# Rows of h carried through the 2x2 scheme of o @ W': four blocks of the second pair

## The chip, the cores and the metric

The kernel runs on one core of one Trainium2 chip. The metric is the device time of one execution in microseconds, as the median over several runs. One core has five engines with instruction queues of their own: TensorE (PE in the profile, with its weight loads as PEld), VectorE (DVE), ScalarE (ACT), GpSimd (POOL) and SyncE (SP). Each works through its own list in the order in which the program wrote it and waits on semaphores for the others. In this kernel SP issues the plain transfers and POOL the accumulating ones, which add what they bring to what lies in the destination.

## The reference

One input x (2048 x 512) goes through two blocks, and a gate of one number per token mixes them:

```
g = sigmoid((x * gate_w).sum(-1))                     # one per token
A: q,k,v = x @ wqkv, 32 heads of 16; phi(t) = where(t>0, t+1, exp(t)) + 1e-6
   kv = sum_s phi(k) v ;  z = sum_s phi(k)
   o  = phi(q) kv / (phi(q) z + 1e-6) ;  a = o @ wo
B: h = (x @ w_gate) * (x @ w_up)                      # 2048 x 1792
   b = h @ w_down                                     # 1792 x 512
out = g * a + (1 - g) * b
```

All of it is in float32. The kernel folds kv into wo, so that `a = o @ W'` where o is phi(q) divided by its denominator (and, in this kernel, multiplied by the gate) and W' is a 512 x 512 matrix.

## The kernel before

**Exactness.** Every operand X of a large matrix product is split into a high part (rounded to the type float32r) and a low part (X minus the high part). A product is then three matmuls, high x high, high x low and low x high (`mm3`, line 60). A split is a ScalarE copy (`act`, L74) for the high part and a VectorE subtraction (`tt`, L77) for the low one. In the names of the profile the letter at the end tells which: `oh` and `ol` for o, `owh` and `owl` for W', `dh` and `dl` for w_down, `hh` and `hl` for h, `wch` and `wcl` for weight combinations.

**Phase 1** computes k, phi(k), the gate and the sum behind kv. It takes about 92 us and isn't touched, but for where the gate's numbers lie.

**Phase 2** goes over two pairs of 512-token chunks (1024 tokens, 8 tiles of 128 tokens, a pair). A pair has 16 units: 14 for the blocks of 128 columns of h (kind "f") and two for q (kind "q", each 256 columns). Units are counted here from 0 to 31 over both pairs. A unit computes two 128-column products for both chunks with seven products instead of eight (a Strassen scheme over a 2x2 split of x and of the weights). In a unit the products stand on TensorE in the order 2 (bank Y), 3 (X), 4 (Y), 1 (R), 5 (X), 6 (R), 7 (S); each is six matmuls 512 wide. Between them VectorE and ScalarE work: R = X - m2, t = R + cross, S = t - X, and at the end of an "f" unit h = R * cross and S * cross, split into hh and hl.

**Fillers.** Between those products stand other matmuls at four places of the unit: ahead of product 4, ahead of product 1, and twice ahead of product 6. `down(k)` puts k down jobs there, and behind them the o jobs that have become ready. `shares` says how many down jobs each place gets (one each where it says nothing).

- A *down job* multiplies one tile of 128 tokens of h, for a group of two neighbouring blocks of h, with w_down: 2 x 3 matmuls 512 wide (`pdn`). VectorE adds the result, times (1 - g), to `acc` (L80). There are 7 groups a pair, so 7 x 8 = 56 jobs.
- An *o job* is one row half of one of seven products of another 2x2 scheme (`OPROD`): o (1024 tokens x 512) and W' are cut into 2 x 2 blocks, and sums of blocks are multiplied. One job is twelve matmuls 256 wide (`po`). VectorE adds the results to the right quarters of `acc`.

**The order of the work around the o jobs** is written by hand in `o_products`. A step of it is one of the places "e" (behind product 3 of a unit), "c" (behind product 4), "t" (behind product 1) and "end" (behind product 7). Counted in steps of job k: the first block of o is loaded at k - 5 (SP), the further blocks are added by accumulating transfers at k - 3 (POOL), and at k the tile is split (`ready`) and the job queued for the next filler place that comes. For the weights of product p, with k = 2p: load at 2p - 5, add at 2p - 3, split at 2p - 1 (`w_split`).

Within a unit ScalarE's list is: m2, the high part of h of the unit before, the split of w_down, place "e", the copy of Y (`cross<-bY`), place "c", three pieces `wch<-wr` of the next unit's weights, two scalings `wr<-wr` of the weights after those (POOL's add `wr<-in_wgu_add` waits for them), place "t", the copy of X, place "s" (ahead of the last filler), the high part of h, place "end". VectorE has the matching list. Everything is pinned to program order.

**At the end** of the last unit stand the rest of the older down jobs, and then the eight jobs of the last group, the last of which closes each tile of the output.

Of the kernel before, what the change touches and what calls it, by code (L numbers as in the profile page):

```python
# [7 lines left out]
F32 = mybir.dt.float32  # L8
# [23 lines left out]
NH = 4  # L32
HALF = D // 2

# [21 lines left out]
STEPS = ("e", "c", "t", "end")  # L56
# [3 lines left out]
def gated_mix(ctx: ExitStack, tc, xt, xp, x, wqkv, wq, wq_add, wo, wgu, wgu_add, wdn, gate_w, out):  # L60
# [48 lines left out]
    ocol = const.tile([P, NT], F32, name="ocol")  # L109
# [16 lines left out]
    nc.vector.memset(gate[:, NT:2 * NT], 0.0)  # L126
# [14 lines left out]
    gpark = dram.tile([NT, P], F32, name="gpark")  # L141
# [248 lines left out]
    def down(k):  # L390
        for fn in jobs[:k]:
            fn()
        del jobs[:k]
        while ojobs and ojobs[0][0] < passed[0]:
            ojobs.pop(0)[1]()
        passed[0] += 1
# [4 lines left out]
    shares = {2: (0, 1, 1, 1), 3: (1, 0, 1, 0), 4: (1, 0, 1, 0), 7: (1, 1, 0, 1), 8: (1, 0, 1, 0), 9: (1, 1, 0, 1)}  # L401
    shares.update({units: (1, 2, 1, 2), units + 1: (1, 1, 1, 0)})
    shares.update({units + m: v for m, v in ((2, (0, 1, 1, 1)), (3, (1, 0, 1, 0)), (4, (1, 0, 1, 0)),
                                             (5, (1, 1, 0, 1)), (6, (1, 1, 0, 1)), (7, (1, 0, 1, 0)),
                                             (15, (1, 1, 0, 0)))})
# [4 lines left out]
    def unit(n, quad):  # L410
# [38 lines left out]
        do(n, "low")  # L449
        do(n, "e")  # L450
# [31 lines left out]
        if quad:  # L482
            quad(1, 1, bank["R"])
        else:
# [5 lines left out]
        if quad:  # L490
            quad(0, 0, bank["S"])
        else:
# [19 lines left out]

    def hidden():
        return [p2.tile([P, 2, CH], F32R, tag=f"h{v}", name=f"h{v}", bufs=NH) for v in "hl"]

    def down_tiles():
        return [p2.tile([P, D], F32R, tag=f"d{v}", name=f"d{v}", bufs=NH + 1) for v in "hl"]

# [52 lines left out]
    def gate_rows():  # L571
# [3 lines left out]
        for q in range(0, P, 2 * NT):  # L575
            dma(gpark[:, q:q + 2 * NT], some[q:q + NT, 0:2 * NT])
# [44 lines left out]
    left = {(p, i): NF // 2 for p in range(NPAIR) for i in range(TPP)}  # L621
    oleft = [2 * len(OPROD) for _ in range(NPAIR)]

    def down_jobs(pair, group):

        def job(i):
# [6 lines left out]
            first = left[pair, i] == NF // 2  # L633
# [5 lines left out]
            for o in range(0, D, step):  # L639
# [3 lines left out]
                for j, ((hh, hl), w2) in enumerate(group):  # L643
                    mm3(pd, (hh[:, c, sl], hl[:, c, sl]), [v[:, cols] for v in w2], j == 0, j == 1)
# [5 lines left out]
                if ends:  # L650
                    to = nc.gpsimd if pair == 0 else nc.sync
                    tc.keep_in_program_order(to.dma_start(out[t * P:(t + 1) * P, cols], a))

# [279 lines left out]
```

## Time and profile before

| | |
|---|---|
| Median of 3 runs | 601.88 us (601.63 to 601.91) |
| Profiled execution | 601.07 us, of it the span 599.3 us |
| TensorE busy | 594.4 us (99% of the span), 2826 matmuls |
| VectorE, ScalarE, GpSimd busy | 457.2, 326.6, 70.3 us |
| Weight loads (PEld) | 496.0 us, beside the matmuls |
| Transferred | 113.40 MB, mean 189 GB/s |

How to read it: a timeline row gives the start in the span, the duration, the engine, the line, the operation and the tiles, written `out<-in`; behind that, in brackets, how long the engine had been idle and what released it. Durations of matmuls (and of VectorE and ScalarE steps in a row) overlap with those of their neighbours, so the distance from start to start is what one of them costs. A grouped row gives the count, the busy time, the mean duration and the idle time of the engine just before. "DMA to landing" is the time from the issue of a transfer until all of it has arrived.

### The profile page before, as it was taken

To read this page: it belongs to the slowest core of one execution; us is meant where nothing else is said; L and a number is where in the kernel's file an instruction comes from. 1 tells how busy PE (TensorE), PEld (TensorE's weight loads), DVE (VectorE), ACT (ScalarE), POOL (GpSimd) and SP (SyncE) were. 2 spreads that over 40 slices of the span, in tenths; PEclk is the share of its full clock that TensorE was granted. 3 is DMA by queue.
4 is the path that set the end of the run, shared out by engine and by line. 5 is a ranking of instruction groups with operands and counts; after the bars stand their busy time and mean duration, and the time that the engine had idled before them with its cause. 6 is when DMAs were issued, how large, how long until landed. Compare 5 with 4: busy or idle time off the path is not lost.

```text
span 599.3 us, 8138 instructions
## 1 busy us (share of the span) xinstructions
PE 594.4 (99%) x2826; PEld 496.0 (83%) x2826; DVE 457.2 (76%) x726; ACT 326.6 (54%) x569; POOL 70.3 (12%) x90
## 2 busy tenths in 40 slices
PE   8999999999999999999999999999999999999997
PEld 6888888888888888888888888888888888888886
DVE  6977895756787779777789986578768778788955
ACT  3855765579655844546345545955754445353320
POOL 0011100000011110222021121000000022210000
PEclk9999999999999999999999999999999999999999
DMA  8567949656959887999887974677784899965003
GB/s 294 180 194 127 289 102 274 167 167 159 262 135 294 206 211 186 288 267 232 188 179 198 238 202 117 162 177 184 207 215 106 231 249 239 236 174 92 1 1 141
DMA packets 62697, 113.40 MB, mean 189 GB/s; under 512 B 7680, under 2 KB 26624, under 8 KB 62592
## 3 DMA queue, kind: packets, MB, share of 16 engines
q1 hardware_dynamic: 51072, 76.18, 37.9%
q0 software_dynamic: 11296, 36.18, 34.0%
q10 hardware_dynamic: 288, 0.52, 0.3%
q8 instruction: 22, 0.36, 0.2%
q14 instruction: 19, 0.16, 0.1%
HBM read 95.03 MB, written 19.93 MB: 192 GB/s over the span
## 4 chain that ended last, share of the span: by engine, by line
PE 99%; DMA 1%; ACT 0%; DVE 0%; issue 0%
PE pdn L68 25%; PE bR L68 15%; PE bY L68 15%; PE bX L68 15%; PE pk L68 7%; PE bS L68 7%; PE gt L68 7%; PE po L68 7%; DMA wraw<-in_wqkv 1%; PE pw L68 0%; PE pkv L68 0%; ACT wkh L74 0%; DVE acc L80 0%
## 5 line engine op out<-in xcount | busy, mean ns | idle before, releaser
L80 DVE SCALAR_TENSOR_TENSOR acc<-pdn,ocol,acc 128x512 f32<-128x512 f32 (+1 forms) x97 | 71.6, 741 | 27.7 <-PE pdn L68 27.2
L68 PE MATMUL pdn<-dl,hh 128*128 128x512 f32 (+1 forms) x226 | 87.6, 388 | 0.0
L68 PE MATMUL pdn<-dh,hh 128*128 128x512 f32 (+1 forms) x226 | 87.6, 388 | 0.0
L74 ACT ACTIVATE hh<-cross 128x512 fp32r<-128x512 f32 x56 | 35.2, 629 | 96.0 <-DVE cross L77 96.0
L68 PE MATMUL pdn<-dh,hl 128*128 128x512 f32 (+1 forms) x226 | 87.5, 387 | 0.0
L77 DVE TENSOR_TENSOR wcl<-wr,wch 128x512 fp32r<-128x512 f32 (+1 forms) x96 | 73.3, 771 | 1.4 <-ACT wch L74 1.2
L74 ACT ACTIVATE wch<-wr 128x512 fp32r<-128x512 f32 (+1 forms) x96 | 60.2, 695 | 0.5 <-DMA wr<-in_wgu_add 0.5
L101 POOL DMA_DIRECT2D wr<-in_wgu_add x28 | 24.0, 858 | 249.2 <-ACT wr L74 136.0
L68 PE MATMUL bX<-xbh,wcl 128*128 128x512 f32 x128 | 49.8, 389 | 0.0
L68 PE MATMUL bX<-xbl,wch 128*128 128x512 f32 x128 | 49.8, 389 | 0.0
L68 PE MATMUL bX<-xbh,wch 128*128 128x512 f32 x128 | 49.8, 389 | 0.0
L68 PEld LDWEIGHTS pdn<-dh,hl 128*128 128x128 f32 x226 | 42.4, 188 | 8.8
L68 PEld LDWEIGHTS pdn<-dl,hh 128*128 128x128 f32 x226 | 42.5, 188 | 8.5
L68 PEld LDWEIGHTS pdn<-dh,hh 128*128 128x128 f32 x226 | 42.5, 188 | 8.5
L74 ACT ACTIVATE cross<-bY 128x512 f32<-128x512 f32 x32 | 19.1, 597 | 47.9 <-PE bY L68 47.7
L77 DVE TENSOR_TENSOR bR<-bX,m 128x512 f32<-128x512 f32 x32 | 22.3, 698 | 24.0 <-PE bX L68 21.1
L77 DVE TENSOR_TENSOR t<-bR,cross 128x512 f32<-128x512 f32 x32 | 22.1, 690 | 23.8 <-PE bR L68 15.2
L74 ACT ACTIVATE cross<-bX 128x512 f32<-128x512 f32 x32 | 19.1, 597 | 38.2 <-DVE bS L77 38.1
L77 DVE TENSOR_TENSOR hl<-cross,hh 128x512 fp32r<-128x512 f32 x56 | 38.2, 683 | 0.6
L74 ACT ACTIVATE wr<-wr 128x512 f32<-128x512 f32 x64 | 36.6, 621 | 2.0 <-DMA wr<-in_wq 1.9
L77 DVE TENSOR_TENSOR acc<-acc,po 128x512 f32<-128x512 f32 x40 | 26.3, 682 | 7.7 <-PE po L68 7.1
L68 PE MATMUL po<-owh,ol 128*128 128x256 f32 x112 | 31.7, 283 | 0.0
(175 smaller groups left out, 1470.5 us busy)
## 6 DMA issues: line engine op xcount, KB each, us to landing
wr<-in_wgu_add POOLq DMA_DIRECT2D x28, 640.0 KB, 7.6
wr<-in_wgu SPq DMA_DIRECT2D x28, 384.0 KB
wdr<-in_wdn SPq DMA_DIRECT2D x28, 256.0 KB
oraw<-opark POOLq DMA_DIRECT2D x20, 256.0 KB, 7.5
xraw<-in_x SPq DMA_DIRECT2D x16, 256.0 KB
terms<-zq SPq DMA_DIRECT2D x16, 256.0 KB
zt<-terms SPq DMA_DIRECT2D x16, 256.0 KB
rb<-den SPq DMA_DIRECT2D x16, 256.0 KB
```

What stands on the lines that cost most here:

```text
L68: tc.keep_in_program_order(nc.tensor.matmul(*args, **kw))
L74: pin(nc.scalar.activation(dst, src, func, **kw))
L77: pin(nc.vector.tensor_tensor(dst, a, b, op=op))
L80: pin(nc.vector.scalar_tensor_tensor(dst, a, scalar, b, op0=op0, op1=op1))
L101: tc.keep_in_program_order(nc.gpsimd.dma_start(dst, src, accum_op=ALU.add))
```

## The change

Four of the second pair's blocks of h (f = 4 to 7, `MIXED`) no longer go through down jobs. Their 512 columns are a second "o" of the same shape, and their rows of w_down a second "W'"; both go through the same seven products, which accumulate in the same banks. So each of the seven products of the second pair has two h jobs and then two o jobs, 28 instead of 14, and the second pair has 5 groups of down jobs instead of 7 (40 jobs).

- **Units of the mixed blocks** (22 to 25): h is written unsplit to `hraw`, and at place "low" of the next unit VectorE multiplies it with `keep`, (1 - g) broadcast over the partitions (two loads by SP). Its sums of blocks (`h_sum`) and its splits happen at the steps of the jobs.
- **Weights of an h job** are loaded from w_down itself, scaled by -1 on ScalarE where the scheme has a minus sign, and the second block is added by a POOL transfer. There are now 14 weight tiles instead of 7 in the second pair, at the same three steps 2j - 5, 2j - 3 and 2j - 1.
- **Steps**: the second pair has five a unit ("e", "c", "t", "s", "end") instead of four. Its second q unit is unit 21 instead of 22, its first unit 17 instead of 18 ("one place sooner"), and so step 0 lies at place "t" of unit 26 instead of unit 27. The 28 jobs end behind unit 31's "end".
- **Fillers**: `shares` is changed; units 18 and 26 of the second pair have no down job, units 22 and 25 one. The o jobs that are ready are now also put behind R = X - m2 (`o_down`), ahead of the place "e".
- **The end**: the two down jobs behind the last unit's product 7, `down(2)`, are gone, and the o/h jobs of steps 26 and 27 stand there.
- **Places**: h (hh, hl) and w_down (dh, dl in one tile) share nine tiles (`SLOTS`), each taken for the next free use once a group's last job is written, instead of 4 + 4 and 5 + 5 of their own. The split of w_down for the second block of a group moves from place "e" to behind the product of R ("r").
- **Gate**: (1 - g) lies in `gate` beside g, is transposed with it and stored too (8 small transfers instead of 4).

```diff
-NH = 4
+SLOTS = 9
+MIXED = ((), (4, 5, 6, 7))
-STEPS = ("e", "c", "t", "end")
+STEPS = (("e", "c", "t", "end"), ("e", "c", "t", "s", "end"))
...
-    for pair, after in enumerate(((2, 5), (1, 4))):
+    for pair, after in enumerate(((2, 5), (0, 3))):
...
-    shares = {2: (0, 1, 1, 1), 3: (1, 0, 1, 0), 4: (1, 0, 1, 0), 7: (1, 1, 0, 1), 8: (1, 0, 1, 0), 9: (1, 1, 0, 1)}
-    shares.update({units: (1, 2, 1, 2), units + 1: (1, 1, 1, 0)})
...
+    shares = {2: (0, 1, 1, 1), 3: (1, 0, 1, 0), 4: (1, 1, 0, 1), 7: (1, 1, 0, 1), 8: (0, 1, 0, 1), 9: (1, 1, 0, 1)}
+    shares.update({units: (1, 2, 1, 2), units + 1: (0, 1, 0, 1)})
+    shares.update({units + m: (0, 1, 0, int(m not in (6, 9))) for m in range(5, 10)})
...
         tt(bank["R"], bank["X"], m2, ALU.subtract)
         do(n, "low")
+        o_down()
         do(n, "e")
...
+        elif mixed:
+            tt(mixed[:, 1], bank["R"], cross[:, 1], ALU.mult)
...
+        def h_sum(k):
+            p, kind, r = line[k]
+            if kind == "h" and len(OPROD[p][2]) == 2:
+                one, other = OPROD[p][2]
+                tt(raw_tile(k), row(other, r), row(one, r), ALU.subtract if one[0] == "-" else ALU.add)
...
+        def w_sum(j):
+            p, kind, _ = line[2 * j]
+            if kind == "h" and OPROD[p][1][0][0] == "-":
+                act(wt[j], wt[j], scale=-1.0)
             for block in OPROD[p][1][1:]:
-                dma_add(wt[p], wraw[block])
+                dma_add(wt[j], w_block(p, kind, block))
...
+    def keep_scale(pair, m):
+        for c in range(2):
+            h = rows_of_h[pair, m][:, c]
+            tt(h, h, keep[c], ALU.mult)
...
+            mixed = rows_of_h[pair, m] = p2.tile([P, 2, CH], F32, tag="hraw", name="hraw", bufs=4)
+            later(n + 1, "low", lambda pair=pair, m=m: keep_scale(pair, m))
+        elif kind == "f" and half:
+            later(n, "r", down_weights)
...
-    down(2)
     do(n, "low1")
+    down(0)
     down(1)
     do(n, "low0")
     down(len(jobs))
```

More of the change, by code (lines that the diff above doesn't have):

```diff
@@ L741, in load @@
         def load(k):
[L742 to L743 removed]
+            p, kind, i = line[k]
+            if kind == "o":
+                dma(raw_tile(k).rearrange("p (r t) -> p r t", r=2), opark[pair, OPROD[p][2][0]][i])
         def add(k):
[L746 to L751 removed]
@@ L790, in o_products @@
+        last = len(line)
         for k in range(-5, last):
-            if k % 2 and (k + 1) // 2 in range(len(OPROD)):
+            if k % 2 and (k + 1) // 2 in range(last // 2):
                 at_step(k, lambda place, p=(k + 1) // 2: w_split(p))
```

158 lines of the change are left out of this document (106 added, 52 removed).

## The prediction

> **What bounds the kernel now.** I read the page's busy line and slices first, then its chain, then the matmul groups by shape.
>
> ```profile
> span 599.3 us, 8138 instructions
> PE 594.4 (99%) x2826; PEld 496.0 (83%) x2826; DVE 457.2 (76%) x726; ACT 326.6 (54%) x569; POOL 70.3 (12%) x90
> PE   8999999999999999999999999999999999999997
> PE 99%; DMA 1%; ACT 0%; DVE 0%; issue 0%
> L68 PE MATMUL pdn<-dh,hh 128*128 128x512 f32 x222 | 86.5, 389 | 0.0
> L68 PE MATMUL po<-owh,oh 128*128 128x256 f32 x112 | 31.6, 282 | 0.0
> ```
>
> TensorE is never idle between head and tail, and 99% of the chain is TensorE. So matmuls that go away are a gain in full, and any moment in which TensorE waits is a loss in full. The means of 389 and 282 ns are latencies that overlap; the cost of one is its distance to the next start:
>
> ```profile
> 560.05 0.28 PE L68 MATMUL po<-owh,oh 128*128 128x256 f32 x1
> 561.48 0.40 PE L68 MATMUL pdn<-dh,hh 128*128 128x512 f32 x1
> 565.69 0.39 PE L68 MATMUL bS<-xah,wch 128*128 128x512 f32 x1
> 569.77 0.39 PE L68 MATMUL pdn<-dh,hh 128*128 128x512 f32 x1
> ```
>
> Twelve 256-wide matmuls lie between the first two rows: 1.43/12 = 0.119 us each. Eighteen 512-wide ones lie between the last two: 4.08/18 = 0.227 us. So a product of a unit (six) and a down job (six) take 1.36 us each, an o job (twelve narrow ones) 1.43.
>
> **The change, part by part.**
>
> *Matmuls.* Four blocks leave the down jobs: 2 groups x 8 jobs x 6 = 96 wide matmuls, 96 x 0.227 = 21.8 us. Fourteen h jobs of twelve come in: 168 x 0.119 = 20.0 to 20.1 us. Net -1.7 us, all on the path. [...]
>
> *Units without filler.* Units 18, 21, 22 and 24 to 26 lose down jobs, so the next engine has less cover. I cost this at nothing where only the unit's own chain is concerned, because unit 0 of before has no filler either:
>
> ```profile
> 92.36 0.39 PE L68 MATMUL bY<-xah,wch 128*128 128x512 f32 x1
> 101.88 0.39 PE L68 MATMUL bY<-xah,wch 128*128 128x512 f32 x1
> ```
>
> It took 9.52 us = 42 x 0.227: no wait. The shared slots go at nothing with it: a group's last down job stands ahead of R6 on TensorE, and the new h is written behind R6. So do the keep loads. The q units' loads and stores move with them, and the units behind are up to 2.7 us shorter:
>
> ```profile
> L77 DVE TENSOR_TENSOR zt<-zt 128x512 f32<-128x512 f32 x12 | 8.2, 684 | 0.8 <-DMA zt<-terms 0.8
> 497.15 0.68 DVE L77 TENSOR_TENSOR t<-bR,cross 128x512 f32<-128x512 f32 x1
> 497.74 0.68 DVE L77 TENSOR_TENSOR wcl<-wr,wch 128x512 fp32r<-128x512 f32 x1
> ```
>
> VectorE's 0.8 us wait for zt may become 0.8 + 2.7; behind it stands t, which R6 of unit 19 needs 2.7 us (two down jobs) later than the bare chain has it, so 0. VectorE's load: its steps start 0.6 us apart (497.15, 497.74). Keep adds 8, the sums of h 10, the splits of o and W' 14 and 7; 16 sums into acc, 8 h splits and 4 w_down splits go. Units 26 and 27 together get 42 steps, 25 to 26 us, against 27.7 us of TensorE: not the bound, but without slack at job 0.
>
> *The first o/h product of the second pair: the first loss.* In unit 26 the order of the changed program is Y X Y R X, job 0, R, S, with nothing before job 0, where before had two down jobs. The same spot of before is unit 27, ScalarE, VectorE and TensorE:
>
> ```profile
> 493.67 0.39 PE L68 MATMUL pdn<-dh,hh 128*128 128x512 f32 x1
> 493.93 0.60 ACT L74 ACTIVATE cross<-bY 128x512 f32<-128x512 f32 x1 [2.44 <-PE bY L68]
> 495.21 0.63 ACT L74 ACTIVATE owh<-wraw 128x512 fp32r<-128x512 f32 x1 [0.69 <-DMA wraw<-wraw]
> 495.75 1.87 ACT L74 ACTIVATE wch<-wr 128x512 fp32r<-128x512 f32 x3
> 497.53 1.14 ACT L74 ACTIVATE wr<-wr 128x512 f32<-128x512 f32 x2
> 498.57 0.62 ACT L74 ACTIVATE oh<-oraw 128x512 fp32r<-128x512 f32 x1
> 499.22 0.69 DVE L77 TENSOR_TENSOR ol<-oraw,oh 128x512 fp32r<-128x512 f32 x1 [0.79 <-ACT oh L74]
> 500.47 0.28 PE L68 MATMUL po<-owh,oh 128*128 128x256 f32 x1
> ```
>
> The second Y ended at 493.67, ol at 499.91: 6.24 us, of which 0.69 was a DMA wait, so 5.55. ScalarE's order in unit 26 is the same row of seven: cross, owh, three wch, two wr, oh. Between the end of Y and the third matmul of job 0 (the first that reads ol) TensorE has only R, X and two narrow ones: 2.72 + 0.24 = 2.96 us. So it waits at least 5.55 - 2.96 = 2.6 us.
>
> On top comes owh's own wait for the weights, which the shorter units make longer:
>
> ```profile
> 478.97 0.60 ACT L74 ACTIVATE cross<-bY 128x512 f32<-128x512 f32 x1 [0.91 <-PE bY L68]
> 480.50 0.48 SPq L98 DMA_DIRECT2D wraw<-wraw x1
> 482.67 0.86 POOL L101 DMA_DIRECT2D wr<-in_wgu_add  x1 [14.10 <-DVE t L77]
> 484.84 0.86 POOL L101 DMA_DIRECT2D oraw<-opark  x1 [1.31 <-DMA wraw<-wraw]
> 485.48 1.10 POOL L101 DMA_DIRECT2D wraw<-wraw  x1
> DMA to landing us min/median/max: 8.7/8.7/8.7
> DMA to landing us min/median/max: 9.7/9.7/9.7
> DMA to landing us min/median/max: 5.8/5.8/5.8
> ```
>
> The landings are those of the wr add at 482.67, of the wraw add at 485.48 (behind it in POOL's queue: 491.4, then 495.2) and of a wraw add at 497.88 with less ahead. The wr add goes out 3.7 us after the cross copy. Unit 25 of the changed kernel is 8 x 1.36 = 10.9 us long; its cross copy comes at 4.3, the wr add at 8.0. The w load (SP, held behind the last store of o, about 6.2; 484.84 - 480.50 = 4.3 us to arrive) lets the w add go at 10.5. It lands between 10.5 + 5.8 = 16.3 and 8.0 + 8.7 + 1.9 = 18.6 (1.9: half of the 3.8 us between the two landings, as one o add lay between), 5.4 to 7.7 us into unit 26. ScalarE is ready for owh at 4.9. The wait is 0.5 to 2.8 us, and wch, wr and oh, then POOL's next wr add, queue behind it. First stall: 2.6 without it, up to 5.4; I take 4.2.
>
> *The next ones.* Jobs 1 and 2 stand together after X of unit 27. The second weight load takes keep's buffer, so SP holds it (and the loads behind it) till unit 26's keep products are done, 4.2 us in; 4.3 to load and 5.8 to add gives 14.4, and ScalarE's owh, oh and the sign change of the third weight block follow till 16.1. Only then goes that block's add: 5.8 more, 21.9 at best. Its owh, oh and ol (0.5 + 0.6 + 0.7 by the rows above) stand in order ahead of job 3's ol, ready at 23.7 or later; unhindered TensorE would be at job 3's third matmul at 18.1. So the lateness grows to 5.6, up to 7.5 if the wr add is ahead in POOL's queue. With no DMA late the sign change would end at 13.2, and 5.8 + 1.8 more is 20.8: 2.7. Sum of both stalls: 2.7 to 7.5, I take 6.2. From unit 28 on down jobs are back between the products; a step there has 22.2/5 = 4.4 us against 20.8/4 = 5.2 before, so I cost it at 0, at most 2.
>
> *The tail: the second loss.* Before covers the last h with three down jobs (the first at 580.75); the change has jobs 26 and 27 there, and job 27's o is split last:
>
> ```profile
> 579.66 0.69 DVE L77 TENSOR_TENSOR cross<-bR,cross 128x512 f32<-128x512 f32 x1 [0.73 <-ACT cross L74]
> 580.38 0.63 ACT L74 ACTIVATE hh<-cross 128x512 fp32r<-128x512 f32 x1 [0.82 <-DVE cross L77]
> 580.75 0.39 PE L68 MATMUL pdn<-dh,hh 128*128 128x512 f32 x1
> 580.95 0.69 DVE L77 TENSOR_TENSOR cross<-bS,cross 128x512 f32<-128x512 f32 x1 [0.60 <-PE bS L68]
> 581.67 0.63 ACT L74 ACTIVATE hh<-cross 128x512 fp32r<-128x512 f32 x1 [0.66 <-DVE cross L77]
> ```
>
> S ended at 580.75. In the changed order the split of w_down now lies between the two cross products: its copy on ScalarE ends at 581.5, its rest on VectorE at 582.2, cross at 582.8, hh at 583.5, oh at 584.0, ol at 584.7, 4.0 us after S. TensorE has job 26 (1.43) and two matmuls (0.24): it waits 2.3 us. Bounds: 1.2 without the w_down split in between (two steps, 1.1 us), 3 if VectorE is one step behind.
>
> *Sum.* -1.7 + 6.2 + 2.3 = +6.8 us. The profiled execution took 601.07 (span 599.3 and 1.77 around it), 0.81 under the median of 601.88. On the median: 608.7, said as 608.5. Ends: -1.7 + 2.7 + 1.2 = +2.2 (604.0) and -1.7 + 7.5 + 3 + 2 = +10.8 (612.7), with a margin 613.5.
>
> **The rivals.**
>
> *Everything stays covered: faster.* Then only the matmuls count: 601.88 - 1.7 = 600.2. For it: no row of before shows TensorE waiting for o. It decides at job 0 of unit 26: ol must be there 2.96 us after Y's end. The rows give 5.55 with no DMA late, so this needs ScalarE in another order than the program has. 0.09.
>
> *Only one of the two losses shows.* The tail alone: 601.88 - 1.7 + 2.3 = 602.5; the start alone at its low end 603 to 604. For it: VectorE has gaps at the tail (0.60 to 0.73 us in the rows). Against: both are in-order chains of single durations. 0.09, of which 0.05 ends within 0.2%.
>
> *The clock drops after the first stall.* The granted clock in the last moments, 3.1 us after the last matmul, and the first matmuls of the kernel:
>
> ```profile
> 595.90:599.00 3.10, 0.04 (x1) 0.00 (x0) 0.48 (x1) 0.00 (x0) 0.00 (x0) 1.00 0.46 169
> 599.00:599.30 0.30, 0.00 (x0) 0.00 (x0) 0.00 (x0) 0.00 (x0) 0.00 (x0) 0.56 0.00 0
> 1.26 3.59 PE L68 MATMUL warm<-xc1h 128*128 128x512 bf16 x8 [1.26 <-DVE xc1h L124]
> ```
>
> The first eight took 3.59/8 = 0.45 us each against 0.227. If TensorE sits idle for 3.9 us ahead of job 0 in one piece and then runs at that pace for as long, some 9 wide matmuls cost 0.2 more each: 1.8 us, and 610 to 612 if job 3 repeats it. [...] Against: two matmuls of job 0 split the gap, and the idle piece may be 2.6. 0.07, at 611.
>
> *The weight adds are late all through units 28 to 31.* Eight or more of fourteen by 1 us: 617. Against: the spacing is only 15% tighter than in before, which has no wait there. 0.05.
>
> **How the numbers follow.** Forecast 0.70 at 608.5, its own range 604 to 613.5. With the clock case that is 0.77 to 0.81 inside, the rest outside, so the range stays. 0.2% (1.2 us) is about what can be told from no change. Faster 0.09; same 0.05; slower 0.70 + 0.04 + 0.07 + 0.05 = 0.86.
>
> **What would show it.** PE matmuls: 96 wide fewer, 168 narrow more, at the same pitches. In the chain ScalarE and VectorE appear by 1% or more. TensorE's idle rows for po name VectorE's ol or ScalarE's oh: some 4 us at unit 26's job 0, about 2 in unit 27, 2.3 behind the last S. ScalarE's owh waits for wraw. [...]

## The result and the profile after

The changed kernel takes 619.43 us (median of four runs, 617.47 to 621.61) against 601.89 us before: 1.029 times as long, 95% interval 1.0255 to 1.0326. The direction was forecast, the size was not: 608.5 was said, and 619.4 lies outside 604 to 613.5.

The profiled execution is the slowest of the four, 621.61 us. From its page: the span, the busy line, two rows of the slices, the start of the chain, and the groups of matmuls for which TensorE waited.

```profile
span 619.6 us, 8338 instructions
PE 599.4 (97%) x2898; PEld 500.1 (81%) x2898; DVE 461.7 (75%) x736; ACT 332.9 (54%) x580; POOL 76.8 (12%) x95
PE   8999999999999989999999899999998789999987
PEclk9999999999999999999999999999999799999999
PE 86%; DVE 5%; DMA 5%; issue 2%; ACT 2%; ACTq 0%; DVEq 0%; POOLq 0%
L71 PE MATMUL pdn<-slot,slot 128*128 128x512 f32 (+1 forms) x582 | 144.5, 388 | 1.3 <-DVE slot L80 1.3
L71 PE MATMUL po<-owh,oh 128*128 128x256 f32 x168 | 48.4, 288 | 8.9 <-ACT oh L77 8.9
L71 PE MATMUL po<-owh,ol 128*128 128x256 f32 x168 | 48.8, 290 | 3.0 <-DVE ol L80 2.9
```

TensorE was 99% of the chain and is 86%. There are 2898 matmuls instead of 2826, as worked out (96 wide ones fewer, 168 narrow ones more), yet the span is 20.3 us longer. I take the distance from each matmul's start to the next and subtract the pitch of before (0.227 and 0.119 us); what is left is TensorE's wait. By unit, in us, without waits below 0.3:

| Unit | Before | After |
|---|---|---|
| 9 (ahead of product 7) | 0.15 | 2.0 |
| 10 (first down job) | 0 | 1.9 |
| 14 (o job) | 0 | 1.1 |
| 16 (o job) | 0.2 | 2.6 |
| 25 (product 4) | 0 | 0.5 |
| 26 (job 0) | 0 | 5.4 |
| half clock behind it | 0 | 2.9 |
| 27 (job 3 and others) | 0 | 2.9 |
| 29 | 0 | 0.3 |
| 31 (the last h) | 0 | 2.4 |

The sum is 22.0, less 0.35 of before and 1.7 of matmuls: 20.0 of the 20.3 us. So three places lost time: the first pair 7.3, the start of the mixed products 11.7, the end 2.4. The first is in units that the mixed products don't touch at all.

TensorE's waits in the first pair, from the timeline (start, duration, operation, in brackets the idle time and what ended it):

```profile
225.81 0.50 PE L71 MATMUL bS<-xah,wch 128*128 128x512 f32 x1 [1.77 <-DVE bS L80]
231.72 0.50 PE L71 MATMUL pdn<-slot,slot 128*128 128x512 f32 x1 [0.62 <-DVE slot L80]
232.92 0.50 PE L71 MATMUL pdn<-slot,slot 128*128 128x512 f32 x1 [0.70 <-DVE slot L80]
300.32 0.39 PE L71 MATMUL po<-owh,ol 128*128 128x256 f32 x1 [0.87 <-DVE ol L80]
342.27 0.39 PE L71 MATMUL po<-owh,oh 128*128 128x256 f32 x1 [0.33 <-ACT oh L77]
344.28 0.38 PE L71 MATMUL po<-owh,ol 128*128 128x256 f32 x1 [1.51 <-DVE ol L80]
```

What VectorE did ahead of the last of these, and under it the same place of the kernel before:

```profile
339.83 0.68 DVE L80 TENSOR_TENSOR cross<-bR,cross 128x512 f32<-128x512 f32 x1
341.73 0.69 DVE L80 TENSOR_TENSOR slot<-wdr,slot 128x512 fp32r<-128x512 f32 x1 [1.22 <-ACT slot L77]
342.34 0.68 DVE L80 TENSOR_TENSOR cross<-bS,cross 128x512 f32<-128x512 f32 x1
342.94 0.68 DVE L80 TENSOR_TENSOR slot<-cross,slot 128x512 fp32r<-128x512 f32 x1
343.54 0.69 DVE L80 TENSOR_TENSOR ol<-oraw,oh 128x512 fp32r<-128x512 f32 x1
```

```profile
333.32 0.68 DVE L77 TENSOR_TENSOR cross<-bR,cross 128x512 f32<-128x512 f32 x1
335.31 0.68 DVE L77 TENSOR_TENSOR ol<-oraw,oh 128x512 fp32r<-128x512 f32 x1
335.47 0.39 PE L68 MATMUL pdn<-dh,hh 128*128 128x512 f32 x1
337.07 0.28 PE L68 MATMUL po<-owh,ol 128*128 128x256 f32 x1
```

Before, ol began 1.99 us after the cross product of R; it was there at 335.99 and needed at 337.07, so it had 1.08 us to spare. In the changed kernel the split of w_down stands in between and first waits 1.22 us for its own copy: 3.71 us, 1.72 more. And the down job that TensorE did in the meantime (1.36 us) now comes after the o job. 1.72 + 1.36 - 1.08 = 2.0 us: that is most of the wait in unit 16 (0.33 + 1.51 of idle time in the rows; by the distances of starts 2.6, of which 0.2 stood before).

The wait in unit 9 is of another kind. Product 7 waits for VectorE, VectorE for ScalarE, and ScalarE for a block of x that SP loads (first row, the changed kernel):

```profile
222.67 0.63 ACT L77 ACTIVATE cbs<-cbs 128x512 f32<-128x512 f32 x1 [4.79 <-DMA wr<-in_wgu]
222.17 0.63 ACT L77 ACTIVATE cbs<-cbs 128x512 f32<-128x512 f32 x1 [4.84 <-DMA cbs<-in_xp]
```

ScalarE of the kernel before waits 2.90 us for the same load, and TensorE loses 0.15. In the runs below that leave this order as it is, TensorE waits between 0.3 and 2.2 us there. The second row is from v5, further below, whose units 0 to 16 have the order of the kernel before: 2.1 us. So unit 9 can't be put down to the order of the steps alone.

The start, unit 26, on POOL, ScalarE and TensorE:

```profile
469.79 0.85 POOL L104 DMA_DIRECT2D wr<-in_wgu_add  x1 [12.56 <-ACT wr L77]
471.70 1.22 POOL L104 DMA_DIRECT2D wraw<-in_wdn  x1 [1.06 <-DMA wraw<-in_wdn]
479.82 0.63 ACT L77 ACTIVATE owh<-wraw 128x512 fp32r<-128x512 f32 x1 [3.27 <-DMA wraw<-in_wdn]
483.17 0.61 ACT L77 ACTIVATE oh<-oraw 128x512 fp32r<-128x512 f32 x1
483.84 0.58 PE L71 MATMUL po<-owh,oh 128*128 128x256 f32 x1 [5.20 <-ACT oh L77]
488.16 0.61 ACT L77 ACTIVATE wraw<-wraw 128x512 f32<-128x512 f32 x1
489.34 1.20 POOL L104 DMA_DIRECT2D wraw<-in_wdn  x1 [4.05 <-ACT wraw L77]
498.49 0.63 ACT L77 ACTIVATE owh<-wraw 128x512 fp32r<-128x512 f32 x1 [4.92 <-DMA wraw<-in_wdn]
499.69 0.39 PE L71 MATMUL po<-owh,oh 128*128 128x256 f32 x1 [1.66 <-ACT oh L77]
```

The first weight block goes out to be added at 471.70 and is there 8.1 us later; ScalarE waits 3.27 us for it, and the copies of the next unit's weights and two scalings stand between owh and oh. The third block's sign change (488.16) stands behind the second's owh and oh; its add takes 9.1 us to arrive, and job 3 waits for it.

During TensorE's long wait at job 0 the granted clock drops to half. The stretches before, in and behind it (the column ahead of the DMA share is the granted clock):

```profile
471.70:482.70 11.00, 6.94 (x31) 5.42 (x29) 5.58 (x10) 4.59 (x9) 2.98 (x3) 1.00 0.97 242
482.70:489.60 6.90, 5.76 (x19) 4.96 (x20) 4.61 (x8) 3.35 (x7) 1.99 (x3) 0.51 1.09 233
489.60:510.50 20.90, 18.80 (x109) 16.11 (x108) 14.44 (x23) 9.59 (x18) 6.60 (x7) 1.00 0.86 178
```

And the end:

```profile
600.60 0.69 DVE L80 TENSOR_TENSOR slot<-wdr,slot 128x512 fp32r<-128x512 f32 x1 [1.22 <-ACT slot L77]
603.13 0.39 PE L71 MATMUL po<-owh,oh 128*128 128x256 f32 x1 [1.69 <-ACT oh L77]
603.86 0.38 PE L71 MATMUL po<-owh,ol 128*128 128x256 f32 x1 [0.22 <-DVE ol L80]
```

### The profile page after: what moved, and what is told of

It is laid out like the page before. It is cut to its first block, busy times and chain, and to the rows that moved or that the text cites. A ratio compares the mean times of both kernels' runs of the same rounds, so it can differ in the third digit from the quotient of the medians.

```text
span 619.6 us, 8338 instructions
## 1 busy us (share of the span) xinstructions
PE 599.4 (97%) x2898; PEld 500.1 (81%) x2898; DVE 461.7 (75%) x736; ACT 332.9 (54%) x580; POOL 76.8 (12%) x95
## 4 chain that ended last, share of the span: by engine, by line
PE 86%; DVE 5%; DMA 5%; issue 2%; ACT 2%; ACTq 0%; DVEq 0%; POOLq 0%
PE pdn L71 20%; PE bR L71 13%; PE bY L71 13%; PE bX L71 12%; PE po L71 8%; PE pk L71 7%; PE gt L71 7%; PE bS L71 6%; DMA wraw<-wraw 2%; DMA wraw<-in_wdn 1%; DMA wr<-in_wgu 1%; DVE cross L80 1%; DVE ol L80 1%; DMA wraw<-in_wqkv 1%; DVE acc L83 1%
## 5 line engine op out<-in xcount | busy, mean ns | idle before, releaser
L71 PE MATMUL pdn<-slot,slot 128*128 128x512 f32 (+1 forms) x582 | 144.5, 388 | 1.3 <-DVE slot L80 1.3
L71 PEld LDWEIGHTS pdn<-slot,slot 128*128 128x128 f32 x582 | 107.5, 188 | 23.4 <-DVE slot L80 2.1
L83 DVE SCALAR_TENSOR_TENSOR acc<-pdn,gate,acc 128x512 f32<-128x512 f32 (+1 forms) x81 | 59.9, 742 | 23.3 <-PE pdn L71 22.7
L77 ACT ACTIVATE slot<-cross 128x512 fp32r<-128x512 f32 x48 | 30.2, 629 | 77.7 <-DVE cross L80 77.6
L71 PE MATMUL po<-owh,oh 128*128 128x256 f32 x168 | 48.4, 288 | 8.9 <-ACT oh L77 8.9
L71 PE MATMUL po<-owl,oh 128*128 128x256 f32 x168 | 48.0, 286 | 0.0
L71 PEld LDWEIGHTS po<-owh,oh 128*128 128x128 f32 x168 | 32.6, 194 | 11.9 <-ACT oh L77 10.3
L71 PEld LDWEIGHTS po<-owh,ol 128*128 128x128 f32 x168 | 32.5, 194 | 4.3 <-DVE ol L80 4.3
L71 PEld LDWEIGHTS po<-owl,oh 128*128 128x128 f32 x168 | 32.6, 194 | 1.2
L80 DVE TENSOR_TENSOR slot<-cross,slot 128x512 fp32r<-128x512 f32 x48 | 32.7, 682 | 0.1
```

Of the source, the lines that this page charges most:

```text
L71: tc.keep_in_program_order(nc.tensor.matmul(*args, **kw))
L77: pin(nc.scalar.activation(dst, src, func, **kw))
L80: pin(nc.vector.tensor_tensor(dst, a, b, op=op))
L83: pin(nc.vector.scalar_tensor_tensor(dst, a, scalar, b, op0=op0, op1=op1))
```

## The experiments

Each run stands beside the kernel before on its chip (601.4 to 602.0 us). Single runs of one kernel with these waits differ by up to 7 us (w1: 617.46 to 624.53), in part by how often the clock halves (mean clocks there 0.994 and 0.989) and by the wait in unit 9 (0.3 in the trace of v3, 2.1 in that of v5, with the same order up to there), so the verdicts rest on the waits in the traces, and the medians are given beside them.

### How much of it has nothing to do with mixing

`x8_no_mix`: all blocks go through down jobs, the rest of the change stays.

```diff
-MIXED = ((), (4, 5, 6, 7))
+MIXED = ((), ())
-    shares.update({units + m: (0, 1, 0, int(m not in (6, 9))) for m in range(5, 10)})
+    shares.update({units + 5: (0, 1, 0, 1), units + 6: (0, 1, 1, 1), units + 7: (0, 1, 1, 1)})
```

> The changed kernel without the mixed products: all 14 blocks of the second pair go through down jobs again (168 narrow matmuls fewer, 96 wide ones more than in the changed kernel), with fillers in units 21 to 23 near those of the kernel before; shared places, the split of w_down behind product 6, o jobs behind R, the q units one place sooner and the order at the end stay. Theory A (some 7.3 us of the loss lie in the first pair and come from those parts): 609 to 610 us, with the waits of units 9, 10, 14 and 16 in place. Rival B (the loss hangs on the mixed products; what the first pair loses is made good later): 602 to 603.5 us.

613.09 us, 1.019 (1.017 to 1.021). The waits: 1.5, 1.9, 1.1 and 2.6 in units 9, 10, 14 and 16, and 1.1, 1.1 and 1.7 in units 28, 30 and 31, which A had forgotten: the second pair has the same order as the first. So 11.6 us are lost without any mixed product, to parts that I had costed at nothing; by the trace some 6.8 lie in units 9 to 16, as in the changed kernel. The waits in units 28 to 31 aren't in the changed kernel's trace, which has other work there.

### One part at a time, in the kernel before

`x5_before_r` (the split of w_down behind product 6), `x6_before_od` (o jobs behind R), and `w3_before_both`. There are no shared places and no mixed products in these.

```diff
+        if kind == "f" and half:
+            later(n, "r", down_weights)
+        elif kind == "f":
             at.setdefault((n, "e"), []).insert(0, down_weights)
```

```diff
         do(n, "low")
+        o_down()
         do(n, "e")
```

> The kernel before, with one part of the change: the split of w_down of the second block of each group stands behind product 6 of its unit instead of at place e. Theory A (that split is what lies ahead of oh and ol in unit 16, and behind the reciprocal of the denominators in unit 10): waits of about 1.9 us in unit 10 and up to 2.4 in unit 16, 604 to 606 us. Rival B (the waits come from the shared places of h and w_down): as before, 601.9 us.

> The kernel before, with one part of the change: o jobs that are ready stand directly behind R = X - m2, ahead of the unit's first down job. Theory A (in units 14 and 16 the o job then comes before its o is split): a wait of about 1.1 us in unit 14, and less in unit 16 where the split of w_down is not in between: 603 us. Rival B (the waits come from the shared places, or need both parts): as before, 601.9 us.

> The kernel before with two parts of the change together: the split of w_down of a group's second block behind product 6, and o jobs directly behind R. The first alone gave 605.2 us, the second alone 601.7. Theory A (in units 14 and 16, and 28 and 30, the waits need both: the one part brings the o job forward by a down job, the other puts two steps ahead of its o): more than the sum of the two, about 1.1 us more in each of units 14, 28 and 30 and 1.4 more in unit 16: 609 to 610 us. Rival B (the two are independent): 605.4 us.

605.23 us (ratio 1.004 to 1.008), 601.72 us (0.9996 to 1.0018) and 610.82 us (1.013 to 1.018). Alone they cost 3.7 and 0.2 us, together 9.4. The first alone waits 0.8 in unit 9, 1.0 more than before in unit 16, 1.8 in unit 26 and 0.5 in unit 30; the 1.9 in unit 10 that A expected of it didn't come, nor did the 1.1 in unit 14 expected of the second. TensorE's larger waits in the run with both:

```profile
296.90 0.39 PE L68 MATMUL po<-owh,ol 128*128 128x256 f32 x1 [0.86 <-DVE ol L77]
340.65 0.38 PE L68 MATMUL po<-owh,ol 128*128 128x256 f32 x1 [1.50 <-DVE ol L77]
485.61 0.50 PE L68 MATMUL bY<-xc4h,wch 128*128 128x512 f32 x1 [1.47 <-ACT m L74]
517.03 0.39 PE L68 MATMUL po<-owh,ol 128*128 128x256 f32 x1 [0.86 <-DVE ol L77]
560.36 0.38 PE L68 MATMUL po<-owh,ol 128*128 128x256 f32 x1 [1.46 <-DVE ol L77]
```

Those of units 14 and 28 (296.90, 517.03) are in neither of the single runs. In unit 16 the split alone shows

```profile
340.64 0.39 PE L68 MATMUL po<-owh,ol 128*128 128x256 f32 x1 [0.53 <-DVE ol L77]
```

and the o job alone

```profile
335.58 0.39 PE L68 MATMUL po<-owh,ol 128*128 128x256 f32 x1 [0.18 <-DVE ol L77]
```

By the arithmetic above the split alone should cost 1.72 - 1.08 = 0.64 there (measured 0.70 in distance of starts) and the o job alone 1.36 - 1.08 = 0.28 (measured 0.34). Both draw on the same 1.08 us of room. Theory A stands; B (independent, 605.4) falls. The profiled run is 1.5 us above the median: the clock halved once behind the wait in unit 16, which cost 1.6.

The wait in unit 10 was in none of the three. The traces show what else it takes: in the changed kernel unit 4 has three down jobs instead of two, so 24 of them, three whole groups, stand ahead of unit 10 instead of 23. Its first down job is then the first of a new group and needs the split of w_down that now comes late. In x5 VectorE has the same order there, but that job is still the last of the old group. So it is the changed fillers together with the later split; no run tried this pair alone.

`x1_first_pair_o_later` takes one of the two out of the changed kernel: o jobs behind R only from unit 16 on.

```diff
-        o_down()
+        if n >= units:
+            o_down()
```

> The changed kernel, but in the first pair (units 0 to 15) the o job that is ready no longer stands directly behind R = X - m2; it goes behind the next down job, as before the change. Theory A (in the first pair TensorE waits for o because the job was moved ahead of a down job): the wait of 1.1 us at the third matmul of unit 14's first o job goes, 619.4 - 1.1 = 618.3 us; the 2.4 us of unit 16 stay, since nothing was moved there. Theory B (o is late by the split of w_down alone, wherever the job stands): the wait of 1.1 us stays, 619.4 us.

618.41 us; the wait in unit 14 is gone, that in unit 16 is as it was. The 1.0 us in the median is no more than single runs differ by; the trace is the evidence.

### Do nine places force the first pair's loss?

`z1_first_pair` and `w1_first2` mend the order with nine places, `v3_places13` gives the first pair its places back.

The edits of z1, beside the one of x1:

```diff
+        if n in (13, 15):
+            do(n, "end")
         do(n, "r")
...
-        later(n + 5, "s", lambda i=i, k=k: cb_load(i, k))
+        later(n + 5, "c", lambda i=i, k=k: cb_load(i, k))
...
-            later(n, "r", down_weights)
+            at.setdefault((n, "r"), []).insert(0, down_weights)
```

w1 has the first two of these, and in place of the third

```diff
-        later(n + 2, "r", z_end)
-        later(n + 2, "r", recip)
+        later(n + 2, "end", z_end)
+        later(n + 2, "end", recip)
...
+        do(n, "end2")
```

where "end2" holds the split of x for the next pair.

> The changed kernel with four repairs that touch the order of the first pair: the o jobs behind R stand there only from unit 16 on; in units 13 and 15 the split of o for the next job stands ahead of the split of w_down; at the place behind product 6 the split of w_down stands ahead of the reciprocal of the denominators (unit 9); and the loads of x for the next pair stand ahead of the loads of the terms (unit 8). Theory A (the first pair loses 7.3 us through the order of ScalarE, VectorE and SP alone): the waits of units 9, 10, 14 and 16 go, 612 us. Rival B (with nine places the first down job of a group follows its own h so closely that the wait only moves to w_down or to the denominators): 615 us or more.

> The changed kernel with the order of the first pair mended a second time: o jobs behind R only from unit 16 on; in units 13 and 15 the split of o for the next job ahead of the split of w_down, but the split of x for the next pair left where it was; the sum of the denominators and its reciprocal at the end of unit 9 instead of behind product 6; the loads of x ahead of the loads of the terms in unit 8. Theory A (order alone makes the first pair's 7.3 us, and the first repair failed since it put other long steps ahead of h): no wait over 0.5 us in units 8 to 16, 611 to 613 us. Rival B (with nine places the first down job of a group follows its own h so closely that some wait of 1 us or more stays in units 10 and 16 in any order): 615 us or more.

620.49 and 618.71 us. In both the waits of units 9 and 14 went, and others took their place: z1 waited 3.0 in unit 10 and 4.2 in unit 16, w1 1.5 in unit 11 and 3.3 in unit 16. Expected were 612 and 611 to 613 by A; B came out.

In v3 a 0 among the places is one of the four buffers of the mixed h; from unit 18 on these are left out of `free`. `shares` of units 4 and 8 are those of the kernel before.

```diff
-    free = [None] * SLOTS
+    free, extra, only9 = [None] * SLOTS + [0] * 4, [], []
...
-        o_down()
+        if n > units:
+            o_down()
...
-        elif kind == "f" and half:
+        elif kind == "f" and half and n >= units:
```

> The changed kernel with thirteen places for h and w_down until unit 17 (the four buffers that later hold the mixed h are lent out till then), and with them the first pair as in the kernel before: its fillers, the split of w_down at place e, no o jobs behind R up to unit 16. From unit 18 on everything is as in the changed kernel. Theory A (the first pair's loss comes from the order that nine places force): units 0 to 16 as before, 7.5 us less than the changed kernel: 612 us. Rival B (that loss has another source, the gate's further stores or the places themselves): 616 us or more.

614.0 us (611.57 to 616.23), 5.4 less than the changed kernel. In its trace units 0 to 16 are as before: 0.3 in unit 9, 0.2 in unit 16, nothing in 10 and 14. Units 25, 26 and 31 wait as in the changed kernel (5.3 in unit 26, 2.4 in 31); unit 27 waits 1.0 instead of 2.9. The gate's further stores stayed, so they aren't the cause. The run takes back the places, the fillers, the split and the o jobs behind R together and can't tell them apart; with nine places I found no order without a loss. That nine places force the split of w_down to come late (a group's places are only free once the jobs of the group before are written) is argued, not tried.

### The start

`x2_cover26` puts four down jobs into unit 26, one ahead of R and three directly ahead of job 0; they come from units 21 to 25.

```diff
+    shares.update({units + m: (0, 1, 0, 0) for m in range(5, 9)})
+    shares.update({units + 9: (0, 0, 0, 0), units + 10: (0, 1, 1, 2)})
```

> The changed kernel, but of the eight down jobs that it spreads over units 21 to 25, four stand in unit 26, three of them between X and job 0 and one ahead of R (units 21 to 24 keep one each, unit 25 none). Theory A (job 0 has nothing to cover ScalarE's and VectorE's chain and the weight transfer): 5.4 us more of matmuls stand ahead of job 0, the transfer starts 1.4 us later against unit 26, so the wait of 5.4 us falls to about 1.4 and the clock no longer drops (2.9 us): 619.4 - 4.0 - 2.9 = 612.5 us, the wait in unit 27 stays at 2.5. Theory B (POOL's adds are the bound of units 26 and 27, and what is won at job 0 comes back at job 3): only the clock's 2.9 us are won, 616.5 us, and unit 27 waits 6 us.

622.78 us, slower than the changed kernel; both theories missed. Job 0 still waited 3.9, units 22, 23 and 25 waited 2.7 together, and unit 28 began at 510.8, as late as without cover (510.5). The first weight block was there at 481.0 instead of 479.8, so the weights came no sooner, and the clock halved as before.

`x4_no_idle` lets TensorE run twelve matmuls that nobody reads ahead of job 0, 2.7 us of work in place of as much idle time.

```diff
         def job(k):
             p, kind, i = line[k]
+            if pair and k == 0:
+                banks.reverse()
+                idle = psum.tile([P, D], F32, tag=banks[0], name="pidle", bufs=2)
+                for _ in range(12):
+                    mm(idle, xa[0][:, 0, 0:P], xa[0][:, 0], start=True, stop=True)
```

> The changed kernel with twelve 512-wide matmuls more, of data that lies there and into a bank that nobody reads, directly ahead of job 0 of the second pair; they take 2.7 us of the 5.4 in which TensorE waits there. Theory A (the idle time itself lowers the granted clock, and the matmuls behind it run at half pace for some 6 us): no clock drop, granted clock 1.00 throughout, job 0 starts at the same moment as in the changed kernel and the matmuls behind it run at 0.227 us: 619.4 - 2.9 = 616.5 us. Theory B (the matmuls behind the wait are slow because of what else runs then, transfers or reads of the same banks): they stay slow, 619.4 us.

```profile
483.69 0.39 PE L71 MATMUL po<-owh,oh 128*128 128x256 f32 x1 [2.63 <-ACT oh L77]
499.20 0.39 PE L71 MATMUL po<-owh,oh 128*128 128x256 f32 x1 [3.60 <-ACT oh L77]
483.70:488.50 4.80, 4.58 (x25) 3.88 (x26) 3.40 (x6) 2.21 (x4) 1.44 (x2) 1.00 1.07 212
499.80:503.20 3.40, 3.19 (x13) 3.00 (x14) 2.64 (x5) 2.55 (x5) 0.00 (x0) 0.50 0.90 236
```

The clock stayed whole at job 0 (third row), so B is out, and unit 27 began at 488.5 instead of 490.9. But job 3 came when it came: it then waited 3.6 instead of 1.7 (second row), and now the clock halved there (last row, 1.5 us) and once more behind the wait at the end (1.6). Unit 28 began at 511.1, and the time was 622.88. What was won ahead of job 3 was lost at job 3, since the third weight block came no sooner. That holds where the third block lands late: 26.6 us after unit 26 began here, 26.7 in the changed kernel's trace. In x3, w1 and v3 it was there after 23.6 to 24.4 us, and unit 27 waits 1.0 to 1.3 in all. So the half clock at job 0 didn't vanish from the time, it moved, and its net cost isn't known.

`y1_weights_early` moves the weights instead.

```diff
+        if MIXED[pair]:
+            later(n0 - 2, "t", lambda: w_raw(0))
+            later(n0 - 2, "end", lambda: w_sum(0))
         for k in range(-5, last):
+            if k % 2 and (k + 3) // 2 in range(last // 2) and MIXED[pair] and k > -3:
+                at_step(k, lambda place, p=(k + 3) // 2: w_sum(p))
...
-            later(n + 1, "low", lambda pair=pair, m=m: keep_scale(pair, m))
...
         w_load(n + 3)
+        if mixed:
+            keep_scale(pair, m)
```

> The changed kernel, with the weights of the mixed products readied earlier: the first weight block is loaded at place t and completed at the end of unit 24 (two and a half places sooner, ahead of the next add in POOL's queue), each add of weights and its sign change stand first in their step (ahead of the split of the weights before and of the adds of o), and the products with keep stand at the end of their own unit, so that keep's buffers come free for the second and third weight block some 2.5 us sooner. The work is the same. Theory A (the bound of units 26 and 27 is the chain of weights: load, add on POOL, copy on ScalarE): job 0 of unit 26 waits some 2.3 us instead of 5.4, without the half clock behind it (2.9), and unit 27's wait of 2.9 goes: 610.6 us. Rival B (the queues of adds on POOL are full: what is moved ahead delays the adds of o and of the next unit's weights as much): 616 us or more, with waits for ol or wcl in place of oh.

618.56 us, though the waits did what A said: 2.5 in unit 26 (2.3 expected), 1.0 in unit 27, unit 28 began at 505.8, 4.7 us sooner than in the changed kernel's trace (the profiled runs: 617.51 and 621.61). Unit 25 waited 1.9 instead of 0.5 (the products with keep stood ahead of the last steps of o), and the clock halved twice for 3.4 us, in unit 9 and at job 0.

`z2_start` keeps the move of the products with keep for unit 25 alone and puts two down jobs ahead of job 0.

```diff
-    shares.update({units + m: (0, 1, 0, int(m not in (6, 9))) for m in range(5, 10)})
+    shares.update({units + m: (0, 1, 0, int(m == 5)) for m in range(5, 10)})
+    shares[units + 10] = (0, 0, 2, 0)
```

> The changed kernel with an earlier first weight block and weights ahead of o in each step, as in the run with the weights readied early, but the products with keep moved only in unit 25, and two down jobs taken from units 23 and 24 and put ahead of job 0 of unit 26. Theory A (the start is bound by the weights and by the missing cover, and both are given): no wait over 0.5 us in unit 26, about 1 in unit 27, no half clock there: 609.5 us. Rival B (units 23 and 24 need their second filler themselves, as when cover was taken from units 21 to 25): 614 us or more, with new waits in units 23 to 25.

617.41 us, its profiled run 614.06. No half clock, 1.7 in unit 26, but 1.5 in unit 25 and 1.4 in unit 27. The 609.5 of A would have needed all of it; B's bound holds.

`z3_all` is z1, z2 and x3 (below) in one, `w2_all2` is w1, z2 and x3 in one with three steps more:

```diff
+        if n == units + 10:
+            do(n, "t")
         w_add(n + 2)
...
         w_low(n + 1, 2)
+        w_load(n + 3)
...
+        third = (n + 4, "e") if pair and j else (n + 3, "end")
-        for i, (m, place) in enumerate(((n + 3, "s"), (n + 3, "r"), (n + 3, "end"), (n + 4, "e"))):
+        for i, (m, place) in enumerate(((n + 3, "s"), (n + 3, "r"), third, (n + 4, "e"))):
```

> The changed kernel with the repairs of the first pair, of the start and of the end together. Theory A (the three losses are independent of each other and of the mixed products as such): the 1.7 us of matmuls saved remain but for about 1 us of small waits, 600 to 601.5 us, level with the kernel before or a little faster. Rival B (what is made good in one place is given back in the next, since the queues of units 26 to 31 are the bound): 606 us or more.

> The changed kernel with the first pair as in the second repair, the last o split ahead of w_down, the first weight block and the adds of weights earlier, two down jobs ahead of job 0 of unit 26, and three further steps for units 23 to 27: the weights of each unit are loaded one place sooner (ahead of product 6, so ahead of the stores of o in SP's queue), the third of the four stores of o comes after m2 in unit 25, and job 0's o is split ahead of the two scalings in unit 26. Theory A (all that was lost is order in the queues): 601 to 604 us. Rival B (units of 10.9 us are shorter than the round of their own weights, load, scaling, add and copy, so that TensorE waits for wch or wcl in units 25 to 27 whatever stands ahead): 606 us or more, with the waits in units 25 to 27.

615.0 and 614.85 us: A falls in both, B's bounds hold. z3 still waits 2.4, 2.7 and 2.6 in units 25 to 27. In w2 job 0 no longer waits at all, and job 3 does:

```profile
492.40 0.63 ACT L77 ACTIVATE owh<-wraw 128x512 fp32r<-128x512 f32 x1 [5.06 <-DMA wraw<-in_wdn]
493.61 0.58 PE L71 MATMUL po<-owh,oh 128*128 128x256 f32 x1 [3.56 <-ACT oh L77]
```

Its add was issued at 481.31 and took 11 us; an add of 640 KB and three of 256 KB had gone into the same queue since 477.6. The transfer engines' share of w2 in this stretch:

```profile
470.00:480.00 10.00, 10.00 (x51) 8.32 (x50) 7.11 (x12) 5.94 (x11) 2.37 (x4) 1.00 0.99 291
480.00:495.00 15.00, 11.40 (x59) 9.35 (x58) 9.94 (x16) 5.68 (x11) 4.68 (x6) 0.90 1.05 218
```

By these shares (0.99 and 1.05) they are full. The kernel before was as full in the same stretch (0.97 and 1.01 in units 26 and 27), but TensorE had down jobs to do there.

The last three have the thirteen places and the repair of the end; v4 has w2's repairs of the start, v5 those of z2, and v6 is v5 without the adding transfers of the h products' weights:

```diff
             for block in OPROD[p][1][1:]:
-                dma_add(wt[j], w_block(p, kind, block))
+                if kind == "o":
+                    dma_add(wt[j], w_block(p, kind, block))
```

> Thirteen places as in the run of that name, and with them the last o split ahead of w_down, the first weight block and the adds of weights earlier, two down jobs as cover ahead of job 0 of unit 26, the weights of each unit loaded ahead of product 6, the third store of o after m2 and job 0's o ahead of the two scalings. Theory A (the start is bound by transfers, about 5 us stay in units 25 to 27): 605 to 607 us. Rival B (the start's waits were an echo of what the first pair delayed): 601 us.

> As the run with thirteen places and all repairs, but without the last three steps (loads of weights, third store and job 0's o stand where the changed kernel has them). Theory A: 605 us, with 4 to 5 us of waits in units 25 to 27. Rival B: 601 us.

> As v5_all4, but the five accumulating transfers that complete the weights of the h products are left out (so those products use one block of w_down where the sum of two belongs). Theory A (the adding transfers and their queue bound the start): the waits of units 26 and 27 go but for 1 us, 601.5 us or less. Rival B (the start is bound by the units' own weights and by ScalarE's list, and the adds only stand beside it): as v5_all4.

609.62, 610.11 and 607.79 us; none of the three came down to a theory's time. v4 is, level with v5, the fastest of the mixed kernels that leave nothing out, and still 1.3% slower than before (1.011 to 1.015). Its waits: 2.4, 0.8 and 3.6 in units 25 to 27, 0.2 at the end, 1.6 for one half clock. v5 waited 1.4, 1.9 and 2.6 there, and 2.1 in unit 9. Without the adds (v6) unit 27 waits 1.0 instead of 2.6, but units 25 and 26 still 2.0 and 2.6:

```profile
473.26 1.37 ACT L77 ACTIVATE wch<-wr 128x512 fp32r<-128x512 f32 x2 [2.70 <-DMA wr<-in_wgu_add]
475.57 0.61 ACT L77 ACTIVATE oh<-oraw 128x512 fp32r<-128x512 f32 x1
476.24 0.39 PE L71 MATMUL po<-owh,oh 128*128 128x256 f32 x1 [1.76 <-ACT oh L77]
```

So in this order the adds of the h products' weights bind job 3 alone. At job 0 it is now the next unit's own weights: oh stands behind their copies, and those wait 2.70 us for their own add. In unit 25 it is m2 behind the last steps of o. A's 601.5 is refuted, and B's "as v5" is off by the 1.6 us of job 3: several chains of about the same length end here, and taking one away shows the next.

### The end

`x3_tail` splits the last o ahead of the split of w_down.

```diff
+        if n + 1 == len(order):
+            do(n, "end")
         do(n, "r")
```

> The changed kernel, but in the last unit the last o tile is split ahead of w_down's split and of the last product's work, instead of behind both. Theory A (job 27 waits for its own o, which stands last in two in-order lists): the waits of 1.9 and 0.4 us behind the last S go, 619.4 - 2.4 = 617.0 us. Theory B (VectorE's list behind the last S is simply too long, and the first new down job waits instead): the wait moves to the down job, 619.0 us or more.

616.94 us; the wait behind the last S fell from 2.4 to 0.2 us. That is A, by the trace. That the median, too, is within 0.1 us of A's is partly luck, since the traces differ elsewhere by as much: in this one unit 9 waits 1.8 us less than in the changed kernel's, and the clock halves behind unit 16 (1.6).

## Why the prediction was wrong in size

*Matmuls, -1.7.* Right: the counts, and the pitches (0.119 us for the narrow ones, 0.227 for the wide ones); the trace's distances bear out -1.7.

*"Units without filler. ... I cost this at nothing."* Half wrong. I had unit 0 as the witness, but unit 0 has no steps of o in ScalarE's list, and its weights were there long before (their copies began at 73.67 us, its first matmul at 92.36). In units 25 and 26 TensorE waits for both; the wait in unit 25 was 0.5 us, and up to 2.4 where fillers had been taken from units 23 and 24 (z3).

*"The shared slots go at nothing with it."* This is the step that failed worst. I looked at whether a place is free when h is written, and it is. I didn't ask what the split of w_down at its new place is queued ahead of: oh and ol of the next job. And I didn't cost the o jobs behind R, nor the first pair's changed fillers; I named them in the change and gave them no term. In unit 16 the split alone and the o job alone overdraw the 1.08 us of cover only by 0.6 and 0.3; x5, x6 and w3 show that it is one and the same cover. Measured: 7.3 us in the first pair. Of these the 1.1 of unit 14 and the 2.4 of unit 16 are shown by w3 to come from those two parts. The 1.9 of unit 10 come, by comparison of traces, from the split and the fillers. The rest, unit 9, is a late load that differs from run to run; why it is late stays open.

*First loss at job 0: 4.2, of 2.6 to 5.4.* Mechanism right, at the upper end: 5.4. The weights arrived 8.1 us into unit 26 where I had 5.4 to 7.7; the add took 8.1 us to land and not 5.8, with the 640 KB of the add ahead of it in the same queue.

*Next ones: 2.0 more.* Right in place (job 3) and cause (the sign change behind owh and oh, then an add): 2.9 in the profile, 1.0 in other runs of the same order (w1, v3). Both stalls together came to 8.3 in the profile, over my upper end of 7.5: I had let the third block's add land in 5.8 us, and it took 9.1. x4 shows what I missed: where that block lands late these waits aren't a sum, and what TensorE gains ahead of job 3 it loses there.

*The tail: 2.3.* Right, 2.4, and x3 confirms the cause.

*The clock rival, 0.07.* It happened, at 2.9 us where 1.8 were priced, since the clock stayed at 0.51 for 6.9 us and I had let it stay for the 3.9 of the wait. It was not chance: the mean clock is 0.994 in all four runs. What it cost net isn't known (x4).

*"The weight adds are late all through units 28 to 31"* did not happen: 0.3 us. "Everything stays covered" and "Only one of the two losses shows" fell too, since both losses came.

Put together: the terms of the mixed products came to +6.8 and measured 5.4 + 2.9 + 2.4 + 0.5 + 0.3 - 1.7 = 9.8, with the clock 12.7. What was left out of the sum, the first pair, was 7.3.

## What to carry to other kernels

Room ahead of a step is one account: when two edits of one change draw on it, add what they draw before you compare it with what is there, for each place where both meet. An edit that only moves a step deserves the same list as a new one, namely everything that is queued behind it on its engine. And where several chains end at the same job, cover for one of them shows the next: find out when the last of them can be there at the soonest, and cost the place by that.

## What the runs showed of the hardware

In the traces the half clock lasted some 3.4 us (0.50 from 342.3 to 345.7 in x1, from 499.8 to 503.2 in x4, from 225.6 to 229.0 in v5) or some 6.8 us (0.51 over the 6.9 us from 482.7 on in the changed kernel), and far shorter waits than the 3.9 us of the forecast were followed by it. In the run with o later in the first pair the longest wait ahead of it was this one:

```profile
341.60 0.39 PE L71 MATMUL po<-owh,ol 128*128 128x256 f32 x1 [1.50 <-DVE ol L80]
342.30:345.70 3.40, 3.40 (x13) 2.91 (x12) 3.38 (x6) 0.00 (x0) 0.00 (x0) 0.50 0.96 249
```

The same wait in the changed kernel (1.51, quoted above) had no half clock behind it (1.00 from 342.3 to 345.7), nor had the wait of 2.63 us at job 0 of x4. So in these runs the length of the longest wait doesn't tell alone whether half clock follows, and what else decides it was not shown. Behind the wait in x1 the narrow matmuls start 0.21 us apart instead of 0.12, and the six wide ones behind them take 2.46 us (343.36 to 345.82) instead of 1.36: some 1.6 us more in all.

That accounts for a part of how far runs of one kernel with such waits lie apart. In w1 (617.46 to 624.53) the mean clocks of the fastest and the slowest run are 0.994 and 0.989; 0.005 of some 620 us is 3 us of the 7, an estimate from these means. The runs of the kernel before lie within 2.4 us on each chip.
